# A forward long convolution as a software pipeline beside gate/up matmuls, with VectorE's operations held in program order

## The chip, the core and the metric

The kernel runs on one core of a Trainium2 chip. The metric is device time in microseconds for one execution. Five runs of the kernel before gave a median of 2061.96 us (2056.61 to 2076.34).

## What is computed

The reference computes a forward pass and the gradients of all its weights and of its input, for one sequence of S = 2048 positions and D = 1024 channels, in bfloat16. The forward pass, cut to what matters here:

```python
x  = A_q
xn = layernorm(x)                              # over the 1024 channels
k_shift = sum(k_pad[:, t:t + S, :] * shift_k[:, 3 - t] for t in range(4))
kv = k_shift * v
y  = irfft(rfft(kv) * rfft(ssm_k))[:S] + kv * ssm_D     # causal, per channel
s  = xn * y
g  = silu((xn @ w_gate) * (xn @ w_up) @ w_down)         # hidden width F = 3584
out = x + s * g
```

The long convolution is per channel and 2048 taps long. The backward pass (gradients for q, k, v, the two convolution kernels, D and the three weight matrices) takes the larger part of the time, and the change doesn't touch it.

## The kernel before, in words

The kernel works in stages on one core. Each stage has matrix work for TensorE that sets its pace, and a second stream of work, mostly for VectorE, that is fed in between its matmuls.

**The stage around the change** covers about the first 580 us. Its matrix work is the gate/up product: the 3584 hidden columns are cut into 14 weight slabs of 256 columns (for both matrices), each loaded by SP's queue into one of two buffers (`load_slab`, L488). `gu_unit` (L561) takes a slab and up to four blocks of 128 positions. For each block it runs eight matmuls of 512 columns into a PSUM tile (psg, two buffers; L569), and ScalarE copies the result into gut (L571). I call this a block below; the stage has 224 of them. At the end of the unit VectorE multiplies the two halves into hN (L575), GpSimd's queue stores hN to Hd (L576), and a deferred `turn` (L578) transposes it on TensorE (L583), copies it on ScalarE (L584), and stores it to HTd. `flush(5)` (L572) runs such deferred work five blocks later.

In the first 100 us slabs 0 and 1 are run on the rows as the layer norm delivers them, in chunks of 1, 1, 2, 4, 4 and 4 blocks of rows (L691, loop at L712). In this part the four rows of the shift kernel are also broadcast to all partitions (`bcast`, Wbc), and the cosine and sine tables of the transform are built (`build_tables`, L167).

**The convolution** is fed in from slab 2 on (`conv_forward`, L592). It works on eight slabs of 128 channels. For each pair of slabs, `shift` (L614) makes kv on VectorE in two halves: four products with Wbc, three additions, one product with v; the accumulator lies in U buffer 7. For each slab, `main` (L651) then runs:

- `h_rows` (L635): the convolution kernel's rows are transposed on TensorE and scaled on ScalarE to hx;
- `fwd4` (L226) on kv, then on hx: matmuls with the tables (psF, L221), a copy by ScalarE to SP (L236, two buffers), and then sums and differences on VectorE (first W from SP, then KX or HX from W);
- a store of KX to KFd and of HX to HFd, for the backward pass;
- `product` (L301): the complex product on VectorE, into KX;
- `inv_dft` (L335): sums on VectorE from KX back into HX.

`tail` (L668) ends a slab: inverse matmuls on HX (psY, `inv_rows`, L407, L415), a copy by ScalarE to yf (L673), and a store to YFd.

**What sets the order.** Each of these functions is a generator whose yields state how much VectorE work, in microseconds, was just issued. `make_pump` (L431) runs the generator until it has issued the wanted share of the total `F_TOTAL` (L689, 439.2 by its own sum); `tick` (L736) asks for one more 182.4th of it after each block. `staggered` (L450) mixes in the tail of the slab before, once 12 units of the present slab are out. This fixes the order in which the program is traced. A scheduler then orders each engine's instructions by when it expects them to be ready, so VectorE's order may differ from the traced one. `tc.issue_after(x)` is an order edge: what is traced in the block stands behind x on x's engine. All element-wise operations go through the helper `tt` (L198), so that VectorE's rows in the profile all show L199; they are told apart by their tiles.

## Time and profile before

| | before |
|---|---|
| median of five runs | 2061.96 us |
| the profiled execution | 2076.42 us |
| its span, first to last instruction | 2074.6 us |
| TensorE, mean granted clock | 0.979 |
| TensorE busy, 0 to 100 us | 81.5 us |
| TensorE busy, 100 to 582 us | 463.0 of 482 us |
| VectorE busy, 100 to 582 us | 411.4 of 482 us |
| ScalarE busy, 100 to 582 us | 251.3 of 482 us |

The profile is of one execution; the time beside the span in the table is that execution's own, and the 1.8 us between them lie outside the first and last instruction. PE is TensorE, DVE VectorE, ACT ScalarE, POOL GpSimd, SP the queue that issues most loads. In the rows, "out<-in" names the tiles, "xN" the number of instructions, and an arrow behind an idle time names what ended it. "Granted clock" is the share of TensorE's full clock that it was given.

### The profile page before, as it was taken

Reading aid. Unit: us, or ns where it says so; the run is one execution under the profiler, and the core shown is the slowest. Engines: PE = TensorE matmul, PEld = TensorE weight load, DVE = VectorE, ACT = ScalarE, POOL = GpSimd, SP = SyncE. Lnnn points to the kernel's source line nnn. Section 1 sums busy time; section 2 is a strip of 40 time slices with the busy share of each in tenths; the row PEclk is TensorE's granted clock in tenths of the full one; section 3 lists DMA queues with packets and bytes.
Section 4 is the critical chain, followed back from the end, with each engine's and each line's share of the span. In section 5 each row is a group of like instructions: output and inputs, shape, how many; then the busy total and the mean of one; then the engine's idle time right before and its main releaser. Section 6 shows DMA issues by size and latency. Waiting matters only on the chain.

```text
span 2074.6 us, 27733 instructions
## 1 busy us (share of the span) xinstructions
PE 1978.5 (95%) x11288; PEld 1057.3 (51%) x11288; DVE 1411.3 (68%) x1576; ACT 703.3 (34%) x962; POOL 304.5 (15%) x480
## 2 busy tenths in 40 slices
PE   6999999999999999999899899999999699999998
PEld 3455555545544446666555556654444344444443
DVE  6779898988836556887999889897473024434343
ACT  4655554546432233343222222334335001111112
POOL 3322222111112111000111221000000001010100
PEclk9999999999999999999999999999999899999999
DMA  9686656557699988665776676765999999393931
GB/s 297 213 270 220 215 206 219 186 187 248 228 293 291 290 290 255 200 218 198 265 249 202 222 244 218 238 231 164 173 224 177 186 206 224 100 194 98 209 96 56
DMA packets 422528, 440.74 MB, mean 212 GB/s; under 512 B 248960, under 2 KB 336824, under 8 KB 408576
## 3 DMA queue, kind: packets, MB, share of 16 engines
q1 hardware_dynamic: 331488, 203.72, 40.4%
q0 software_dynamic: 42112, 176.51, 25.5%
q10 hardware_dynamic: 48800, 58.73, 8.8%
q8 instruction: 88, 1.44, 0.3%
q14 instruction: 40, 0.33, 0.1%
HBM read 198.72 MB, written 189.83 MB: 187 GB/s over the span
## 4 chain that ended last, share of the span: by engine, by line
PE 39%; issue 30%; DVE 17%; DMA 6%; POOL 5%; ACT 2%; SPq 0%; POOLq 0%; ACTq 0%; DVEq 0%
PE psx L1224 16%; PE psb L1201 7%; PE psb L1100 6%; PE psg L569 5%; DVE W L199 5%; DVE m L199 3%; PE psb L1085 2%; DVE HX L199 2%; PE psF L221 1%; DVE A L199 1%; DVE U L199 1%; DMA B<-HFd 1%; DVE KX L199 1%; DVE B L199 1%; POOL out_dram L64 1%
## 5 line engine op out<-in xcount | busy, mean ns | idle before, releaser
L569 PE MATMUL psg<-wslab,U 128*128 128x512 bf16 x1792 | 419.1, 387 | 8.5 <-ACT U L542 5.0
L1100 PE MATMUL psb<-U,U 128*128 128x512 bf16 x1792 | 399.3, 383 | 13.4 <-DVE U L199 13.4
L1224 PE MATMUL psx<-U,dgut 128*128 128x512 bf16 x1536 | 339.3, 382 | 19.6 <-ACT wbs L1203 14.8
L1224 PEld LDWEIGHTS <-dgut 128*128 128x128 bf16 x1792 | 174.8, 98 | 233.3 <-issue 28.0
L1100 PEld LDWEIGHTS <-U 128*128 128x128 bf16 x1792 | 176.5, 99 | 224.0 <-issue 23.0
L569 PEld LDWEIGHTS <-U 128*128 128x128 bf16 x1792 | 175.8, 100 | 203.4 <-issue 18.3
L1085 PE MATMUL psb<-wdt,U 128*128 128x256 bf16 x1792 | 200.7, 273 | 1.1 <-ACT bm L979 1.1
L571 ACT CAST gut<-psg 128x512 bf16<-128x512 f32 x224 | 131.4, 587 | 206.5 <-PE psg L569 195.6
L1201 PE MATMUL psb<-U,U 128*128 128x512 bf16 x896 | 194.9, 379 | 6.0 <-ACT wbs L1203 4.4
L1085 PEld LDWEIGHTS <-U 128*128 128x128 bf16 x1792 | 176.0, 98 | 25.2 <-issue 1.4
L961 PE MATMUL psbm<-U,ht 128*128 128x512 bf16 x784 | 169.9, 379 | 0.0
L1105 ACT CAST wb<-psb 128x512 bf16<-128x512 f32 x112 | 66.4, 596 | 302.8 <-PE psb L1100 282.8
L199 DVE TENSOR_TENSOR W<-SP 128x1024 f32<-128x1024 f32 x96 | 113.0, 1220 | 69.4 <-ACT SP L236 37.8
L1201 PEld LDWEIGHTS <-U 128*128 128x128 bf16 x896 | 87.3, 98 | 111.1 <-issue 3.7
L199 DVE TENSOR_TENSOR dka<-dkh,Wbc 128x1024 bf16<-128x1024 bf16 x16 | 11.1, 692 | 193.0 <-DMA dkh<-DKSHd 193.0
L199 DVE TENSOR_TENSOR W<-W 128x1024 f32<-128x1024 f32 (+1 forms) x144 | 139.1, 984 | 2.8
L1247 ACT ACTIVATE dx_t<-dxn 128x1024 bf16<-128x1024 f32 (+1 forms) x17 | 17.1, 1007 | 348.8 <-DVE dxn L199 291.4
L199 DVE TENSOR_TENSOR m<-A,B 128x2048 bf16<-128x2048 bf16 (+1 forms) x48 | 73.2, 1575 | 84.1 <-issue 33.2
L961 PEld LDWEIGHTS <-ht 128*128 128x128 bf16 x784 | 76.6, 98 | 91.8
L1087 ACT CAST dht<-psb 128x512 bf16<-128x512 f32 x112 | 65.3, 586 | 130.3 <-PE psb L1085 110.1
L1203 ACT CAST wbs<-psb 128x512 bf16<-128x512 f32 x56 | 33.4, 622 | 146.6 <-PE psb L1201 80.8
L199 DVE TENSOR_TENSOR U<-U,dht 128x2048 bf16<-128x2048 bf16 x56 | 68.2, 1218 | 15.8 <-ACT dht L1087 15.8
(202 smaller groups left out, 2302.2 us busy)
## 6 DMA issues: line engine op xcount, KB each, us to landing
U<-GUd SPq DMA_DIRECT2D x28, 1024.0 KB, 7.3
DGd<-U SPq DMA_DIRECT2D x28, 1024.0 KB, 5.2
GUd<-gut ACTq DMA_DIRECT2D x54, 512.0 KB, 4.4
A<-DYFd POOLq DMA_DIRECT2D x16, 1024.0 KB, 6.6
out_dram<-wb ACTq DMA_DIRECT2D x112, 128.0 KB, 3.4
U<-Hd ACTq DMA_DIRECT2D x14, 1024.0 KB, 7.2
Hd<-hN POOLq DMA_DIRECT2D x54, 256.0 KB, 4.0
HTd<-hT POOLq DMA_DIRECT2D x54, 256.0 KB, 4.1
```

Of the source, the lines that this page charges most:

```text
L64: return nc.gpsimd.dma_start(out=out, in_=in_)
L199: V.tensor_tensor(o, a, b, op)
L569: gu_mm[0] = nc.tensor.matmul(ps[:], XNT[q][:, dc, qi * P:(qi + 1) * P], w[:, dc].rearrange("p a f -> p (a f)"), start=(dc == 0), stop=(dc ...
L571: nc.scalar.copy(out=gut[:, :, i], in_=ps[:].rearrange("p (a f) -> p a f", a=2))
L961: nc.tensor.matmul(ps[:, dh * 512:(dh + 1) * 512], ht(fc)[:, i * P:(i + 1) * P], WD[fc // 4][:, fc % 4, dh * 512:(dh + 1) * 512], start=(f ...
L1085: nc.tensor.matmul(ps[:, x * SLW:(x + 1) * SLW], DBMT[2 * hf + g][:, dc, (b % 4) * P:(b % 4 + 1) * P], wdt[:, dc, :], start=(dc == 0), sto ...
L1087: nc.scalar.copy(out=dht[:, 2 * e:2 * e + 2].rearrange("p b f -> p (b f)"), in_=ps[:])
L1100: nc.tensor.matmul(ps[:], XN[b // 4][:, b % 4, dc * P:(dc + 1) * P], dgus[b // 8][:, :, b % 8], start=(b == 0), stop=(b == NB - 1))
L1105: nc.scalar.copy(out=wb[:, dc % 2].rearrange("p a f -> p (a f)"), in_=ps[:])
L1201: nc.tensor.matmul(ps[:], h[:, b, f * P:(f + 1) * P], DBM[b // 4][:, b % 4, dh * 512:(dh + 1) * 512], start=(b == 0), stop=(b == NB - 1))
L1203: nc.scalar.copy(out=wbs[:, dh * 512:(dh + 1) * 512], in_=ps[:])
L1224: nc.tensor.matmul(ps[:, dh * 512:(dh + 1) * 512], t[n][:, f, i * P:(i + 1) * P], WGU[n][:, f, dh * 512:(dh + 1) * 512], start=(n == 0 and ...
```

## The change

1. VectorE is held in program order while the convolution runs: with `PIN[0]` set, every `tt` gets an order edge to the instruction traced before it on VectorE. It is set after the first shift product and cleared at the end of the stage.
2. `fwd4` is cut into `fwd4_half` (matmuls and ScalarE's copy of one half), `fwd4_sums` and `fwd4_outs` (VectorE). In the new loop the matmul halves are issued ahead: those of hx while VectorE works on kv's sums, those of the next slab's kv during the inverse sums (`ahead`).
3. The tail's four row pairs are issued one by one at fixed places in the next slab (`next(tl, None)`); the next slab's `h_rows` is issued before HX's last sums. `staggered` is no longer used here.
4. The shift product of the next pair stands between `product` and `inv_dft` of the odd slab, and the two halves of it use different accumulators (U 7 and U 6).
5. The first shift product (20 units) runs before slab 2; the rest is spread over the blocks. The statement of the work is new too (`F_TOTAL` 440.8).
6. hN is multiplied one block later, behind the copy of the next block, and its store and its turn are issued from there.
7. With the last two chunks of rows the order of the units is (4, slab 0), (5, slab 0), (4, slab 1), (5, slab 1) where it was (4, 0), (4, 1), (5, 0), (5, 1).

On SP's queue the order of one load changes: HT0[1][:, 0:8] from HTd now stands ahead of the pair of loads of slab 13. Behind the stage, all engines' orders stay as they were.

The core of the diff:

```diff
+    PIN = [False]
     def tt(o, a, b, op):
-        V.tensor_tensor(o, a, b, op)
+        ins = V.tensor_tensor(o, a, b, op)
+        if PIN[0]:
+            tc.keep_in_program_order(ins)
...
+    def fwd4_half(x, i, wp, psp, first=None):
+        SP = wp.tile([P, 2, 2, 512], F32, name="SP", bufs=2)
+        for par in range(2):
+            ps = psp.tile([P, 2, 2, 256], F32, name="psF")
+            cmm(ps[:, 0], T4[par], x, (i, i + 4), first if i == 0 else None)
+            cmm(ps[:, 1], T4[par], x, (i + 2, i + 6))
+            nc.scalar.copy(out=SP[:, :, par], in_=ps[:].rearrange("p s k x -> p s (k x)"))
+        return SP
+    def fwd4_sums(W, SP, i):
+        s, q = [SP[:, j].rearrange("p a (k x) -> p (a k) x", k=2) for j in range(2)]
+        tt(W[:, 0, i], s, q, ADD)
+        tt(W[:, 1, i], s, q, SUB)
...
             flush(5)
+            hn[0]()
+            hn[0] = nop
             tick()
         sta(GUd[sl, b0 // 8][:, :, b0 % 8:b0 % 8 + n], gut[:, :, 0:n])
-        tt(hN[:, 0:n], gut[:, 0, 0:n], gut[:, 1, 0:n], MUL)
-        st(Hd[sl][:, b0:b0 + n, :], hN[:, 0:n])
+        def multiply():
+            tt(hN[:, 0:n], gut[:, 0, 0:n], gut[:, 1, 0:n], MUL)
+            st(Hd[sl][:, b0:b0 + n, :], hN[:, 0:n])
+            defer(turn)
+        hn[0] = multiply
...
-                acc = U[7][:, 0:2048].rearrange("p (e r d) -> p e r d", e=2, r=8)
+                acc = U[7 - c][:, 0:2048].rearrange("p (e r d) -> p e r d", e=2, r=8)
...
+        yield from shift(0)
+        PIN[0] = True
+        yield 6.0
+        h_rows(0)
+        tl = iter(())
+        sp = [fwd4_half(kvs(0), i, cs, ps_cv) for i in range(2)]
         for ds in range(8):
-            yield from staggered(main(ds), tl, 12.0)
+            yield 0.5
+            W = fwd4_buf(cs)
+            fwd4_sums(W, sp[0], 0)
+            yield 2.4
+            fwd4_sums(W, sp[1], 1)
+            D0 = S_.pop(("D", ds))[:]
+            sph = [fwd4_half(S_["hx"], 0, cs, ps_cv, D0)]
+            yield 2.4
+            KX = cx.tile([P, 16, 256], BF16, name="KX")
+            fwd4_outs(KX, W, 0)
+            sph.append(fwd4_half(S_["hx"], 1, cs, ps_cv, D0))
+            yield 2.4
+            fwd4_outs(KX, W, 1)
+            st(KFd[ds], KX[:])
+            next(tl, None)
+            yield 2.4
+            W = fwd4_buf(cs)
+            for i in range(2):
+                fwd4_sums(W, sph[i], i)
+                next(tl, None)
+                yield 2.4
+            if ds < 7:
+                h_rows(ds + 1)
+            HX = cs.tile([P, 16, 256], BF16, name="HX", bufs=2)
+            for i in range(2):
+                fwd4_outs(HX, W, i)
+                next(tl, None)
+                yield 2.4
+            turned(HX, 1, 0, 1)
+            yield 1.3
+            st(HFd[ds], HX[:])
+            yield from product(KX, HX, KX, cs, False, 0)
+            if ds % 2 == 1 and ds < 7:
+                yield from shift(ds // 2 + 1)
+            sp = []
+            def ahead():
+                if ds < 7:
+                    sp.append(fwd4_half(kvs(ds + 1), len(sp), cs, ps_cv))
+            ahead()
+            yield from inv_dft(KX, HX, cs, ahead)
+            S_["G", ds] = HX
             tl = tail(ds)
...
-        for sl in range(2):
-            gu_unit(sl, b0, n, slabs[sl], nop)
-            if i in (3, 4):
+        for i_, sl in ([(i, 0), (i, 1)] if i < 4 else ([(4, 0)], [(5, 0), (4, 1), (5, 1)])[i - 4]):
+            gu_unit(sl, *xs[i_][0:2], slabs[sl], nop)
+            if i_ in (3, 4):
                 with tc.issue_after(gu_mm[0].ins):
-                    for j in ((3,), (2,), (1,), (0,))[2 * (i - 3) + sl]:
-                        bcast(j)
+                    bcast((3, 2, 1, 0)[2 * (i_ - 3) + sl])
...
     def tick():
         cnt[0] += 1
-        pump(cnt[0] / NT)
+        pump((20.0 + (F_TOTAL - 20.0) * cnt[0] / NT) / F_TOTAL)
+    pump(20.0 / F_TOTAL)
```

## The prediction

> **What bounds the kernel now.** I read the page first. TensorE is busy almost always, so time can only be won where it waits or runs at less than its full clock.

> ```profile
> PE 1978.5 (95%) x11288; PEld 1057.3 (51%) x11288; DVE 1411.3 (68%) x1576; ACT 703.3 (34%) x962; POOL 304.5 (15%) x480
> ```

> Nearly all the edits lie in the forward convolution, which shares 100 to 582 us with the gate/up matmuls (L569). So next: who TensorE waited for in that stretch.

> ```profile
> engine line waited for: us in total, times, longest us
> PE psY L415 <- DVE HX L199: 13.9, 5, 4.4
> PE psg L569 <- DMA wslab<-in_B_w_gate_dram: 3.0, 1, 3.0
> PE tr L583 <- ACT hT L584: 1.1, 1, 1.1
> PE tr L583 <- DVE hN L199: 0.8, 1, 0.8
> ```

> Two entries matter: the inverse transform's matmuls (psY) wait for VectorE's HX, and slab 2 of the weights once comes late. TensorE's timeline around one HX wait shows that the wait isn't all of it.

> ```profile
> 219.96 0.60 PE L415 MATMUL psY<-HX,TI 128*128 128x256 bf16 x4 [0.53 <-DVE HX L199]
> 220.39 2.97 PE L569 MATMUL psg<-wslab,U 128*128 128x512 bf16 x13
> 227.30 1.01 PE L415 MATMUL psY<-HX,TI 128*128 128x256 bf16 x4 [3.94 <-DVE HX L199]
> 230.67 1.91 PE L415 MATMUL psY<-HX,TI 128*128 128x256 bf16 x8
> 234.99 1.03 PE L415 MATMUL psY<-HX,TI 128*128 128x256 bf16 x8
> ```

> Eight of these matmuls take 1.91 us after the wait and 1.03 us a little later: half clock. The clock column (before "DMA share") of 7 us windows after the four long waits gives the price:

> ```profile
> 227.00:234.00 7.00, 6.70 (x35) 4.32 (x35) 6.86 (x7) 2.77 (x4) 2.78 (x5) 0.61 0.22 76
> 342.00:349.00 7.00, 6.15 (x24) 3.22 (x24) 6.84 (x6) 1.66 (x3) 0.09 (x1) 0.54 0.20 72
> 456.00:463.00 7.00, 7.00 (x31) 3.99 (x31) 0.21 (x1) 2.35 (x4) 0.00 (x0) 0.63 0.11 36
> 103.00:110.00 7.00, 6.79 (x31) 3.04 (x32) 2.62 (x3) 2.09 (x3) 2.36 (x4) 0.77 1.09 351
> ```

> 7 x (0.39 + 0.46 + 0.37 + 0.23) = 10.2 us. With the waits, 13.9 + 3.0, the two causes cost 27 us. That is nearly all that this change can win between 100 and 582 us; what lies behind 582 us keeps its order.

> **Durations.** I cost the change by start-to-start steps read from the timeline of before. TensorE: 0.216 us for 512 columns (32 of L569 last 7.07 us), 0.109 to 0.114 for 256, 0.056 for a transpose. VectorE: these rows (the last two figures ahead of "idle": busy us, mean ns).

> ```profile
> L199 DVE TENSOR_TENSOR W<-SP 128x1024 f32<-128x1024 f32 x64 | 75.1, 1219 | 37.9 <-ACT SP L236 37.8
> L199 DVE TENSOR_TENSOR HX<-W 128x1024 bf16<-128x1024 f32 x64 | 74.8, 1218 | 0.3
> L199 DVE TENSOR_TENSOR W<-KX 128x2048 f32<-128x2048 bf16 x16 | 36.6, 2287 | 0.3
> L199 DVE TENSOR_TENSOR U<-k,Wbc 128x2048 bf16<-128x2048 bf16 x24 | 29.3, 1220 | 6.2 <-DMA KSHd<-U 5.9
> ```

> Successive ones overlap by some 0.08 us (two HX<-W take 2.35 us), so a step is 1.14 us, 1.2 to 1.27 where the next needs it, 2.2 to 2.26 for the double ones, 0.60 for hN and turned.

> **Program order on VectorE, and the split of the forward transform.** No operation is added or removed, so each engine's work is unchanged. Two slabs of channels and one shift product take VectorE about 2 x 40.4 + 19.5 + 11.5 hN x 0.60 = 107 us. TensorE has 46 blocks of 8 x 0.216 = 79.5, psF and psY 192 x 0.11 = 21.5, and transposes and D rows 7.5 in the same span: 108.5 us. The engines are evenly matched; what decides is the order.

> The compiled order tells why before waits: psY of slabs 0 to 7 stands at blocks 65, 83, 110, 129, 156, 174, 202, 215, alternately 18 and 27 apart, while VectorE finishes HX every 57 us, since its scheduler spread the shift product over both slabs. From HX 0 to HX 1 VectorE needs 57 us, TensorE about 41. So I added each queue up in its order, with the steps above, stopping VectorE where hN or SP isn't there yet, and TensorE at HX. For before, HX leads psY by +10.5, -5.7, +8.7, -4.5, +8.3, -5.2, +9.9, -1.4 us. The trace waited 4.5 (0.53 + 3.94), 4.1, 4.4 and 0.8 us at the four negative ones and nowhere else. The sum is right in place and 0.4 to 1.2 us too pessimistic.

> For the changed order (psY at blocks 57, 84, 103, 131, 149, 177, 195, 213; the shift product now in one piece, so both engines have the long gap at the same place) the same sum gives +8.3, +7.7, +10.8, +8.6, +9.9, +9.4, +10.8, +1.5. Every HX wait goes: 13.9 us, and with it 7 x (0.39 + 0.46 + 0.37) = 8.5 us of clock.

> What is late next: the pipeline issues psF of the next slab's kv directly behind the shift product. On TensorE's order it comes 1.9, 2.2 and 1.9 us before VectorE has kv (slabs 2, 4, 6), and about 1.9 us at slab 0. Behind these psF matmuls in TensorE's queue stand gate/up blocks, so everything waits. Less the pessimism of 0.7 each: 4 x 1.3 = 5 us. The copy of hx's SP half waits until VectorE has read the kv half two before (two buffers); that comes out at 0.1 us three times, nothing.

> What no row shows is whether a wait of 1.3 us halves the clock. The nearest rows: waits of 0.8 to 1.1 us were followed by none, one of 2.96 us was (eight matmuls in 3.33 us where 1.89 is usual). [...] By the row the threshold is below 3 us, and each may cost up to 3.2 us more (the clock lost after an HX wait): 5 to 18 us. A gain is excluded, a wait can't speed anything. I take 7.5, near the short waits, with one of the four hit.

> **hN a block later, turn with it.** 54 multiplies, same work. They are traced behind the next block's copy, so VectorE's queue meets gut already copied; behind a waiting hN stand the convolution's sums, and in the sum above hN stops VectorE by at most 2.3 us. The transposes follow six blocks later (14 us); hN is at most 8 us late. The Hd and HTd stores move past KFd, HFd and YFd on GpSimd's queue. KFd and HFd must land (4.4 and 5.9 us) before VectorE overwrites KX and HX; the tightest, slab 2's HFd behind YFd and a turn, lands some 5 us before. Nothing, either way; if that cover is gone, VectorE stalls by the excess.

> **First shift product ahead of the pace; new pace.** 20 of 440.8 units run before slab 2, the rest at 2.31 instead of 2.41 per block. Its work hides beside the tables. Row 0 of the broadcast weights comes four blocks later, which is what makes the first kv late by 1.9 us (counted). The second accumulator (U 6) removes the KSHd wait of 5.9 us on VectorE, which was not on TensorE's path.

> **Slab 0 finished sooner.** Its last block moves from 28 to 24, so slab 2's load is issued 4 x 8 x 0.216 = 6.9 us sooner. It landed at 103.2 and was needed at 100.2; now about 96.3. Gone: 3.0 + 7 x 0.23 = 4.6 us. The fifth chunk of four rows is now needed at about 74.6 us, and its last transposed copy ended at 71.2, so it is there. If it weren't, each us would show.

> **HTd ahead of slab 13 on SP's queue.** That load now stands before slab 13's pair and waits for a turn at block 190; slab 13's buffer is free at 192 and it is needed at 200, 17 us later. It lands in 12 to 14. Covered by 3 to 5 us; without the cover, it is the excess plus the half clock, as at 103 us.

> **The sum.** 27.0 - 7.5 = 19.5. The profiled execution, 2076.4 us, would become 2056.9. The median of before is 14.5 us lower than that execution; I take the same difference off it: 2062.0 - 19.5 = 2042.5.

> **The rivals.**
> A, the forecast: 2036 to 2049, chance 0.57.
> B, no new wait: kv is in time, since the sum is pessimistic. Gain 27, 2035. For it: VectorE's waits for SP in before (37.8 us in all), which halves issued ahead can fill. Against it: four negative sums. 0.18.
> C, every kv wait halves the clock: 27 - 18 = 9, 2053; or the slab is all that is gained, 2057. For it: the 2.96 us row. 0.18.
> D, slower: VectorE, now strictly in order, becomes the bound. One operation that waits holds all behind it, and psF, hence the gate/up blocks, wait for kv at every second slab. It decides once VectorE's 107 us per two slabs grow by over 27 / 3.5 = 7.7 us (115 us); at 118 us it loses 10 us net, 2072. For it: 85% of VectorE is busy in the stage already (411 of 482 us). Against: no operation there showed more than 1.27 us. 0.07.

> Measurement tells about 0.5% from no change, 10 us: faster is below 2051.7. A and B lie there, with part of C: faster 0.80, same 0.14, slower 0.06. The range takes in B and most of C, with the spread of before's runs (2056.6 to 2076.3): 2030 to 2056.

> **What would show it.** Right: no psY wait for HX; the slab wait gone; psF waits for kv of 1 to 2 us at slabs 0, 2, 4 and 6; clock 0.99 or more between 100 and 582 us; stage shorter by about 20 us. Wrong: psF waits of 3 us or more with half clock behind them (C), VectorE busy without gaps over 95% (D), ScalarE's SP copies waiting for VectorE, or a wait for wslab near block 200.

## The result

The kernel after took 2061.14 us (median of 44 executions, 2039.46 to 2086.21) where the kernel before took 2069.62 (79 executions, 2049.04 to 2107.97) on the same chip. The ratio is 0.9955, 95% interval 0.9937 to 0.9974: 9 us gained, 5 to 13. The forecast was 2042.5 us and a gain of 19.5. The ratios leave out executions more than 1.5% above the fastest of their kernel; the means and standard deviations below are over all of them, and "either way" gives a 95% interval. The two means are 10.1 us apart, 4.5 either way.

The profiled execution of after took 2058.03 us, with a span of 2056.0. Its first row, which answers to the first line shown of before:

```profile
PE 1969.4 (96%) x11288; PEld 1053.4 (51%) x11288; DVE 1415.3 (69%) x1576; ACT 703.4 (34%) x962; POOL 305.0 (15%) x480
```

TensorE is busy 9 us less than in before (1978.5), with the same 11288 instructions. Eight psY matmuls of before took 1.91 us at half clock and 1.03 at full, so less busy time for the same work is clock won: the mean granted clock is 0.983 here, 0.979 in before. TensorE's waits in the forward stage, up to 582 us, as line, awaited operation, total, number of times, longest:

```profile
engine line waited for: us in total, times, longest us
...
PE psF L225 <- DVE kv L201: 6.4, 4, 2.2
...
PE tr L600 <- DVE hN L201: 1.3, 1, 1.3
PE tr L600 <- ACT hT L601: 1.1, 1, 1.1
PE psF L225 <- ACT SP L237: 0.5, 2, 0.3
```

No psY row waits for HX any more (13.9 us in before), and none waits for wslab (3.0). What is new is the first row, psF waiting for kv: 6.4 us in four waits, none over 2.2. The forecast had the place and the size (5 us, 1 to 2 each). TensorE's timeline at slab 2, then the stage and the 7 us after each long kv wait (TensorE's granted clock is the figure ahead of DMA share and GB/s):

```profile
209.83 2.42 PE L225 MATMUL psF<-kv,TF 128*128 128x256 bf16 x16 [1.97 <-DVE kv L201]
212.04 0.63 PE L580 MATMUL psg<-wslab,U 128*128 128x512 bf16 x1
212.46 2.90 PE L225 MATMUL psF<-kv,TF 128*128 128x256 bf16 x16
```

```profile
100.00:582.00 482.00, 472.28 (x2930) 265.08 (x2929) 416.51 (x366) 252.36 (x354) 106.59 (x163) 1.00 0.69 229
207.00:214.00 7.00, 5.03 (x29) 3.33 (x28) 6.90 (x7) 2.95 (x4) 4.64 (x7) 0.79 0.74 236
321.00:328.00 7.00, 4.82 (x38) 3.56 (x37) 6.90 (x6) 3.10 (x4) 3.54 (x6) 1.00 0.96 321
432.00:439.00 7.00, 5.03 (x39) 3.65 (x38) 6.90 (x7) 3.55 (x5) 2.00 (x3) 1.00 0.42 152
```

One of the three waits (207 us) is followed by half clock, two are not. Over 100 to 582 us the clock is 1.00 (0.98 in before) and TensorE is busy for 472.28 us (462.96 in before), so it does more of the work inside this window: the last gate/up matmul starts at 561.0 us, 578.1 in before. The stage gained 17.1 us in this pair of profiles. Nothing in the diff touches what comes behind, yet the measured gain of the kernel is 9. So two questions were open: how much the stage gains in an ordinary execution, and whether the rest takes some of it back.

### The profile page after: what moved, and what is told of

Read it like the earlier page. It is cut to its first block, busy times and chain, and to the rows that moved or that the text cites. A ratio compares the mean times of both kernels' runs of the same rounds, so it can differ in the third digit from the quotient of the medians.

```text
span 2056.0 us, 27710 instructions
## 1 busy us (share of the span) xinstructions
PE 1969.4 (96%) x11288; PEld 1053.4 (51%) x11288; DVE 1415.3 (69%) x1576; ACT 703.4 (34%) x962; POOL 305.0 (15%) x480
## 4 chain that ended last, share of the span: by engine, by line
PE 58%; DVE 18%; issue 11%; DMA 6%; SPq 3%; POOL 2%; ACT 2%; ACTq 0%; POOLq 0%; DVEq 0%
PE psx L1277 19%; PE psg L580 12%; PE psb L1153 8%; PE psb L1254 7%; DVE W L201 4%; DVE U L201 4%; DVE m L201 3%; PE psb L1138 3%; PE psF L225 3%; PE psbm L1014 2%; DVE A L201 2%; DMA out_dram<-wbs 2%; SPq L1220 1%; PE psY L423 1%; SPq L1213 1%
## 5 line engine op out<-in xcount | busy, mean ns | idle before, releaser
L580 PE MATMUL psg<-wslab,U 128*128 128x512 bf16 x1792 | 414.5, 383 | 4.8 <-ACT U L550 4.3
L1277 PE MATMUL psx<-U,dgut 128*128 128x512 bf16 x1536 | 340.3, 383 | 14.3 <-ACT wbs L1256 11.0
L1300 ACT ACTIVATE dx_t<-dxn 128x1024 bf16<-128x1024 f32 (+1 forms) x17 | 17.1, 1007 | 347.5 <-DVE dxn L201 293.2
L201 DVE TENSOR_TENSOR W<-SP 128x1024 f32<-128x1024 f32 x96 | 112.4, 1220 | 33.2 <-ACT SP L276 28.3
L201 DVE TENSOR_TENSOR U<-U,dht 128x2048 bf16<-128x2048 bf16 x56 | 68.2, 1218 | 15.1 <-ACT dht L1140 15.1
```

What stands on the lines that cost most here:

```text
L201: ins = V.tensor_tensor(o, a, b, op)
L580: gu_mm[0] = nc.tensor.matmul(ps[:], XNT[q][:, dc, qi * P:(qi + 1) * P], w[:, dc].rearrange("p a f -> p (a f)"), start=(dc == 0), stop=(dc ...
L1277: nc.tensor.matmul(ps[:, dh * 512:(dh + 1) * 512], t[n][:, f, i * P:(i + 1) * P], WGU[n][:, f, dh * 512:(dh + 1) * 512], start=(n == 0 and ...
```

## The experiments

Three theories stood at the start. **Theory 1**: the stage gains its 17 us in every execution, and the rest is spread of later stages. **Theory 2**: the profiled execution of before lost unusually much in this stage. **Theory 3**: the later stages give some 8 us back, because the change moves them against something. The runs fall into five groups, each on a chip of its own beside executions of before: both kernels again, slab 0's order and kv's psF later in the code; the forward stage and the eight buffers; plain loads and ScalarE's queue; the next three experiments; the last one. The mean of before was 2067.7, 2069.3, 2077.1, 2070.1 and 2064.2 us there.

**Both kernels again, unchanged.** No edit.

> The kernel before, unchanged, for a second profile. Theory 1 (the forward stage is 17 us shorter in every execution; the rest of the median's shortfall is spread of the later stages, which the change doesn't touch): the last gate/up matmul lies at 578 to 583 us again, with psY waits for HX of about 14 us in all, and the parts behind it differ from the first profile by up to 10 us either way. Theory 2 (the first profile showed an unusually bad forward stage): the last gate/up matmul lies at 573 us or sooner. Ratio 1.00.

Measured: 2072.86 us (12 executions, 2047.29 to 2095.45; ratio to the other executions of before 1.0021, 0.9978 to 1.0063). Last gate/up matmul at 579.5 us.

> The changed kernel, unchanged. Theory 1: the last gate/up matmul at 561 to 566 us again, psF waits for kv of 6 to 7 us, and later parts that differ from the first profile by up to 10 us either way; ratio anywhere from 0.988 to 0.999, about 17 us on the mean of many. Theory 2: the stage is at 563 us again but the kernel before comes closer to it. Theory 3 (the later stages lose what the forward stage won, because the change moves them against something): the parts behind the forward stage are longer by some 8 us than those of the kernel before in the same call.

Measured: 2051.3 us (12 executions, 2043.7 to 2083.14; ratio 0.9935, 0.9894 to 0.9975). Last gate/up matmul at 562.7 us. So the profiles repeat to 1.7 us in the forward stage, while whole executions of one kernel differ by up to 60 us. TensorE's waits behind 582 us show where, first in the first profile of after, then in its second:

```profile
PE psb L1254 <- ACT wbs L1256: 14.1, 1, 14.1
...
PE psx L1277 <- ACT wbs L1256: 11.0, 1, 11.0
```

```profile
PE psx L1277 <- ACT wbs L1256: 5.5, 1, 5.5
...
PE psb L1254 <- ACT wbs L1256: 2.3, 1, 2.3
```

These rows belong to the down-projection's weight gradient and the dx stage behind it: 25 us of waits in one execution, 8 in the other, of the same kernel (19 in the first profile of before). The change doesn't touch these stages.

**Slab 0's new order alone.** In before, only the loop over the last units is replaced:

```
-        for sl in range(2):
-            gu_unit(sl, b0, n, slabs[sl], nop)
+        for i_, sl in ([(i, 0), (i, 1)] if i < 4 else ([(4, 0)], [(5, 0), (4, 1), (5, 1)])[i - 4]):
+            gu_unit(sl, *xs[i_][0:2], slabs[sl], nop)
```

> The kernel before with nothing but the new order of the units of the last two chunks of rows (the last slab-0 unit ahead of a slab-1 unit). By the prediction: the wait for slab 2 is gone and with it 3.0 us and 1.6 us of clock, 4.6 us in all; the psY waits stay at about 14 us. Ratio 0.998. Rival: the later chunk of rows isn't ready or the broadcast row is late, and nothing is won.

Measured: 2069.5 us (ratio 0.9976, 0.993 to 1.0022). The wait for wslab is gone from its profile, the HX waits are all there (14.8 us). Its last gate/up matmul starts at 570.5 us, but a gain of a few us can't be told from the times in this spread.

**kv's psF later in the code.** In after, its two halves are called inside the inverse transform instead of ahead of it, and row 0 of the broadcast weights comes earlier:

```
-            ahead()
-            yield from inv_dft(KX, HX, cs, ahead)
+            yield from inv_dft(KX, HX, cs, ahead, ahead)
...
```

> The changed kernel with the next slab's kv matmuls issued two steps later (behind the first and the second half of the inverse sums) and the last broadcast row one unit sooner. By theory: the psF waits for kv (6.4 us in the profile of the changed kernel) go, with some 2 us of clock, and the forward stage ends at 554 to 558 us. Rival: VectorE then waits for SP at the head of the next slab by as much, HX comes later, and psY or psF waits come back: stage at 562 us or more.

Measured: 2052.3 us (ratio 0.9951, 0.9911 to 0.9991). The three long kv waits stayed at 6.1 us, and the stage ended at 559.8 us, not at 554 to 558. The compiled order tells why: psF of slab 2's kv stands behind block 78.9 in both kernels, since the scheduler places TensorE's instructions by its own estimate of when kv is ready. The edit moved lines of code and not the instruction, so it tells nothing about the three waits.

**The forward stage by itself.** Both kernels end behind the stage; the backward half is left out.

```
     for p_ in (ps_cv, ps_y, ps_tr, ps_gu, fg, fw):
         p_.release()
+    for p_ in (ua, tfp, tip):
+        p_.release()
+    return
```

> The kernel before, ended after the forward stage (its last gate/up block, transposes and stores); the backward half is left out, so that only outputs of the forward half are written. Two profiles of the whole kernel before have their last gate/up block at 578.1 and 579.6 us, so about 585 to 590 us here with the last turn and stores. This and the next run are a pair. Theory 1 (the forward stage gains the 17 us of the profiles in every execution, and the smaller gain of the whole kernel, 9.9 us between all 126 executions of before and all 56 of after, is the spread of the later stages): this is 16 to 18 us above its pair, and executions of it spread by few us. Theory 2 (the profiled executions of before lost unusually much in this stage): this is only 8 to 11 us above its pair. Theory 3 (the later stages give 7 to 8 us back): 16 to 18 us above its pair, as in theory 1; the other pair tells these two apart.

> The kernel after, ended at the same place, with the same part left out. Two profiles of the whole kernel after have the last gate/up block at 561.0 and 562.7 us. Theory 1 and theory 3: 16 to 18 us below its pair. Theory 2: 8 to 11 us below.

Measured: 586.73 us (5 executions, 580.57 to 588.28) and 572.19 us (4 executions, 570.58 to 573.61). The means are 13.0 us apart, 4.4 either way. Theory 2 has a part of the truth: the profiled pair of the whole kernels, with 17.1, was at the upper end. The waits of the forward-only profiles are those of the whole kernels (13.9 us for HX and 2.6 for wslab in one, 6.4 for kv in the other). What varies is the start: the 257th gate/up matmul comes at 98.2 us here, at 103.2 in the first profile of before.

**More buffers for the weight gradient's rows.** wbs is what TensorE waited for behind 582 us, so both kernels got eight buffers instead of four:

```
-    wo = pool("wo", 4, side="right")
+    wo = pool("wo", 8, side="right")
```

> The kernel before with 8 instead of 4 buffers for the rows of the down-projection's weight gradient on their way out (wbs), and no other edit; the order of every engine stays as it was. In six profiles the stage that fills them takes 207 to 236 us, and TensorE waits there for wbs for 0 to 24 us, since its stores stand behind transposing loads on SP's queue. If that is where executions differ, this kernel has its stage at 205 to 212 us, its median lies some 10 us below before's (about 2052 to 2060), and its executions spread less than before's (standard deviation about 12 us). If not, median and spread stay.

> The kernel after with the same 8 buffers. Theory 1 (the spread of the later stages hides the gain): with that spread cut, this is 16 to 18 us below its pair. Theory 2 (before's forward stage usually loses less than in its profiles) and theory 3 (the later stages give back 7 to 8 us): 8 to 11 us below its pair. Theory 3 has its loss in this stage, or where dx waits for it: then it is gone with the buffers, and the pair differs by 16 to 18 us only if both are measured at equal medians of the other stages.

Measured: 2056.77 us (10 executions, standard deviation 25; ratio to before 0.992, 0.9877 to 0.9963) and 2068.91 (12 executions, 13; ratio 0.9987, 0.9941 to 1.0032). The means are 3.3 us apart, 19 either way, and by the two ratios the order is even the reverse: the pair decides nothing, and the spread has not shrunk. The profile of the second shows that with more buffers TensorE waits for another late transfer, and still for wbs. First TensorE's timeline, then the load of the DMA queues from 1480 to 1530 us (queue, packets, MB, share of the 16 engines' time; then issues: transfer, KB, median us to landing):

```profile
1529.33 6.11 PE L1254 MATMUL psb<-U,U 128*128 128x512 bf16 x16 [15.68 <-DMA U<-Hd]
1545.64 4.85 PE L1254 MATMUL psb<-U,U 128*128 128x512 bf16 x11 [10.20 <-ACT wbs L1256]
```

```profile
q1 hardware_dynamic: 5104, 2.13, 72.7%
...
U<-Hd ACTq DMA_DIRECT2D x2, 1024.0 KB, 41.3
...
out_dram<-wbs SPq DMA_DIRECT2D x2, 256.0 KB, 42.0
```

Queue 1 carries what SP issues, the transposing loads of w_gate and w_up and the stores of wbs. It moves 2.13 MB in 50 us and takes 72.7% of the engines' time for it. Beside that, a load of 1 MB on ScalarE's queue (Hd) takes 41.3 us to land, and a store of wbs 42.0.

**The same loads made plain.** They bring the same bytes without transposing, so dx gets untransposed operands; the work and order of TensorE, VectorE, ScalarE and GpSimd are the same. In both kernels, and likewise for DGd:

```
-        nc.sync.dma_start_transpose(out=store, in_=(B_w_gate, B_w_up)[a][:, j * 512:(j + 1) * 512])
+        ld(store.rearrange("p a (h f) -> p (a h) f", f=512),
+           (B_w_gate, B_w_up)[a][:, j * 512:(j + 1) * 512].rearrange("(p x) f -> p x f", p=P))
```

> The kernel before with the transposing loads of w_gate, w_up and DGd for the last two stages made plain loads of the same bytes, so dx gets untransposed operands; order and work of TensorE, VectorE, ScalarE and GpSimd stay. In the profiles one such load holds SP's queue for 15 to 47 us while rows of a weight gradient and with them TensorE wait. If these loads are the source of the spread, the stage of the down-projection's weight gradient takes 200 to 206 us, executions differ by less than 5 us (standard deviation) and the median lies near 2030 to 2045. This and the next are a pair that compares the two kernels with little spread. Theory 1 (the gain of the forward stage reaches the end): 13 to 17 us above its pair. Theory 3 (later stages give some back whatever their spread): 8 to 10 us above. Theory 2, that the profiles of before are unusual, is weakened by the forward pair (13.1 us between the means, 11.8 to 16.7 between profiles).

> The kernel after with the same loads made plain. Theory 1: 13 to 17 us below its pair. Theory 3: 8 to 10 us below, and its dw, down-projection gradient or dx stage is longer than its pair's by the rest. Were it equal to its pair or slower, all theories would fall.

Measured: 2041.69 us (6 executions, standard deviation 4.7) and 2028.35 (6 executions, 2.8). The means are 12.8 us apart, 5.1 either way. Most of the spread is gone, and with it 29 us of the mean time of before (2069.8 over all its executions; 36, 8 either way, against those on this chip). The last gate/up matmuls of the two profiles are 12.3 us apart (574.5 and 562.2), the ends 13.1. Here are the last 603 us ahead of the final stores (us, busy time of PE and so on, with PE's clock third from the end), first of before's kernel, then of after's:

```profile
1427.00:1630.00 203.00, 202.99 (x1067) 96.97 (x1066) 107.54 (x106) 77.06 (x80) 8.22 (x14) 1.00 0.71 224
1630.00:2030.00 400.00, 399.62 (x2019) 184.17 (x2017) 155.31 (x207) 54.58 (x79) 38.54 (x61) 1.00 0.46 145
```

```profile
1414.00:1617.00 203.00, 202.99 (x1067) 96.94 (x1065) 107.44 (x106) 77.06 (x80) 8.22 (x14) 1.00 0.71 224
1617.00:2017.00 400.00, 399.49 (x2018) 184.04 (x2016) 155.83 (x207) 54.58 (x79) 38.53 (x61) 1.00 0.47 145
```

TensorE is busy for 202.99 of 203 us in both, at full clock. The same 13 us lie between the windows as lie between the kernels. So theory 3 falls where the transposing loads are taken out: nothing behind the stage gives anything back that shows. Theory 1 holds with 13 us in the place of 17.

**The stores of wbs on ScalarE's queue**, in both kernels, with the transposing loads as they were:

```
-            wst = ld(o_dwd[f0:f0 + P, :], wbs)
+            wst = sta(o_dwd[f0:f0 + P, :], wbs)
```

> The kernel before with the stores of wbs issued from ScalarE's queue instead of SP's, so that none stands behind a transposing load; nothing else edited (ScalarE's copies of yl move by a few places). If the spread of the later stages is this queueing, TensorE's waits for wbs (0 to 24 us) go, the median lies 8 to 15 us below before's, and the spread is cut. If the transposing loads slow all transfers, wbs or U<-Hd waits stay and so do median and spread.

> The kernel after with the same stores moved to ScalarE's queue. Theory 1: 13 to 17 us below its pair, at about 2040 if the queueing was the cause of the spread. Theory 3: 8 to 10 us below its pair. If all of this holds it is the fastest kernel so far.

Measured: 2082.22 us (ratio to before 1.0073, 1.0041 to 1.0105) and 2071.47 (ratio 1.0008, 0.9971 to 1.0046). The means are 13.0 us apart, 8.7 either way, as theory 1 had it. But the edit made nothing faster: the ratio of the first puts it 0.4 to 1.0% above before on the same chip (the means are 7.2 us apart, 8.9 either way), and TensorE waits 36 us for wbs in either. So a place in SP's queue is not all that the stores wait for. Around TensorE's longest wait for wbs in the first profile (17.3 us, to 1633.8), two loads of 352 KB on GpSimd's queue take 31 us beside transposing loads of DGd; over the whole profile their medians are 4.9 and 5.5. Whether the stores also stand behind the loads of Hd on ScalarE's queue was not tested.

With plain loads, single terms of the sum could be weighed, though against the plain pair on another chip: differences of 2 or 3 us decide little.

**Slab 0's order, plain loads** (the edit of the slab run above).

> The kernel before with plain loads (dx gets untransposed operands, as in the pair before) and the new order of slab 0's last units alone. If the slab's term was right (4.6 us), the median is about 2037 where the kernel before with plain loads had 2041.7; if only the late slab itself counts (waits of 2.6 to 3.3 us, mostly without half clock behind them), 2038.5 to 2039.5. The HX waits of 13.9 us stay, since nothing of the convolution is moved; psY's blocks stay at 65, 83, 110, 129.

Measured: 2038.84 us; the means are 2.2 us below the plain kernel before, 5.8 either way. The wait of 2.7 us for wslab is gone from the profile, and the last gate/up matmul starts 1.5 us sooner (573.0). The forecast's 4.6 is not excluded, half of it is nearer.

**After without VectorE's program order, plain loads.**

```
-        PIN[0] = True
+        PIN[0] = False
```

> The kernel after with plain loads, but VectorE's operations left to the scheduler (it mixes the last shift product's multiplies with the next channels' sums again; psY stays at blocks 57, 84, 103, 131, psF of kv moves from 79 to 77). If the program order is what removes the HX waits, they are back at every second slab, and the median is 2035 to 2042; if the pipelining and the shift product in one place do it, HX waits stay at zero, and the median is 2027 to 2031, or below 2027 if the order itself costs something.

Measured: 2030.56 us; the means are 2.3 us above the plain kernel after, 3.1 either way. TensorE's waits of the stage:

```profile
PE psF L225 <- ACT SP L237: 3.8, 1, 3.8
PE psF L225 <- DVE kv L201: 3.2, 1, 3.2
PE tr L600 <- DVE hN L201: 2.3, 1, 2.3
PE psY L423 <- DVE HX L201: 2.0, 1, 2.0
```

HX is late once (2.0 us), not 13.9 us in five waits. So most of the HX waits go with the rest of the change, whether or not the scheduler may shuffle VectorE. Nor is it the shift product in one piece: here VectorE spreads it over two slabs again, as in before (six of its products start between 165.0 and 233.8 us, in among the sums), and HX is in time everywhere else. What does differ from before in both kernels is how long VectorE waits for ScalarE's copies into SP, between 100 and 582 us: 37.8 us in before, and here in after and then without the order:

```profile
DVE W L201 <- ACT SP L237: 4.0, 1, 4.0
```

```profile
DVE W L201 <- ACT SP L237: 11.9, 7, 3.3
```

This points to the matmul halves issued ahead, but no run takes them out alone. Holding the order is worth some 2 us (the last gate/up matmul starts at 565.2 us without it, at 562.2 with it), and the interval reaches nought. Without it kv is late at slab 0 alone, so its three long waits come with the order.

**kv's psF really later.** In after, for slabs 2, 4 and 6, psF of kv comes behind the inverse transform, tied to VectorE's last operation there (`LAST[0]`, which `tt` keeps); it moves from block 78.9 to 81.0 at slab 2.

```
-            ahead()
-            yield from inv_dft(KX, HX, cs, ahead)
+            def late():
+                with tc.issue_after(LAST[0].ins):
+                    ahead()
+            if ds % 2 == 1 and ds < 7:
+                yield from inv_dft(KX, HX, cs)
+                late()
+                late()
+            else:
+                ahead()
+                yield from inv_dft(KX, HX, cs, ahead)
```

> The real kernel after with psF of the next slab's kv issued behind the inverse transform's last operation on VectorE at slabs 2, 4 and 6, so it stands 1.4 to 2.1 blocks (2.5 to 4 us) later in TensorE's order; VectorE's order is unchanged. The psF waits for kv (6.4 us in four) fall to under 1 us, and nothing takes their place, since VectorE needs the result some 4 blocks later. The forward stage ends at 552 to 556 us instead of 561 to 563. The whole kernel: 6 to 9 us below after, within a spread of 12 us; it is the candidate for the fastest.

> The same edit with plain loads. If the waits for kv cost what their time and the clock behind them add up to (6.4 plus 1.7 to 3.4 us), the median is 2019 to 2022, where the kernel after with plain loads had 2028.4. If VectorE is what paces the stage by then, so that a wait removed here comes back as a wait for HX, the median stays at 2026 to 2029.

Measured: the real kernel 2046.96 us (6 executions; ratio to before 0.9897, 0.9843 to 0.9951), with plain loads 2029.42. The plain means are 0.6 us above the plain kernel after, 4.2 either way. The gain expected of the real kernel's stage didn't come: it ends at 561.7 us (562.4 with plain loads), not at 552 to 556. As the other case had it, the wait came back, though at SP and not at HX. The waits of the plain profile, and the instructions around one:

```profile
PE psF L226 <- ACT SP L238: 7.3, 3, 2.6
...
PE psF L226 <- DVE kv L202: 0.3, 1, 0.3
```

```profile
219.34 4.62 DVE L202 TENSOR_TENSOR W<-SP 128x1024 f32<-128x1024 f32 x4
...
221.80 1.93 ACT L238 COPY SP<-psF 128x1024 f32<-128x1024 f32 x2 [4.18 <-DVE W L202]
222.87 3.26 PE L226 MATMUL psF<-hx,TF 128*128 128x256 bf16 x16 [2.34 <-ACT SP L238]
```

kv is late by 0.3 us in all, and psF of hx waits 7.3 us in three waits instead. ScalarE's copy into SP stands idle for 4.18 us until VectorE has read (W<-SP) the SP half two before. There are two SP buffers, and VectorE comes to that half only behind the shift product.

**The second half of hx later too.** On top of the last edit, for slabs 2, 4 and 6, this half moves from block 83 to 86:

```
-            sph.append(fwd4_half(S_["hx"], 1, cs, ps_cv, D0))
+            if ds not in (2, 4, 6):
+                sph.append(fwd4_half(S_["hx"], 1, cs, ps_cv, D0))
...
+            if ds in (2, 4, 6):
+                with tc.issue_after(LAST[0].ins):
+                    sph.append(fwd4_half(S_["hx"], 1, cs, ps_cv, D0))
```

> The kernel with psF of kv behind, and psF of the second half of hx 3 blocks later too (block 83 to 86 at slab 2, likewise at 4 and 6); VectorE's order is unchanged. If only the places were too early, the SP waits of 7.3 us go, no other comes (HX led psY by 8 to 11 us in the sum along the queues), and the forward stage ends at 553 to 556 us. If VectorE paces the stage, psY waits for HX instead and the stage still ends at 561 to 563. The whole kernel: in the first case 15 to 22 us below before, in the second as the kernel after.

> The same with plain loads. First case: median 2018 to 2022 (the kernel after with plain loads had 2028.4). Second case: 2026 to 2029.

Measured: the real kernel 2048.34 us (8 executions; ratio to before 0.9912, 0.9873 to 0.995), with plain loads 2023.53. The plain means are 3.0 us below the plain kernel after, 4.9 either way. The SP waits are gone, and a third wait has come (one of the four, of 0.2 us, lies in the first 100 us):

```profile
PE psg L581 <- ACT gut L583: 5.9, 4, 2.5
```

```profile
332.20 4.63 DVE L202 TENSOR_TENSOR W<-SP 128x1024 f32<-128x1024 f32 x4
...
334.65 1.93 ACT L238 COPY SP<-psF 128x1024 f32<-128x1024 f32 x2 [5.58 <-PE tr L601]
336.46 1.09 ACT L583 CAST gut<-psg 128x512 bf16<-128x512 f32 x2
...
337.12 0.59 PE L581 MATMUL psg<-wslab,U 128*128 128x512 bf16 x1 [2.50 <-ACT gut L583]
```

ScalarE's copy into SP still waits for VectorE. The profile names a transpose as its releaser, but it starts 2.45 us after W<-SP began, as in the profile above (2.46 us, 219.34 to 221.80), which is when two of the four W<-SP are done. The copy of the gate/up result (gut), which follows it on ScalarE, comes at 336.46, so the gate/up matmuls wait 2.50 us. Neither of the two cases was quite met: the stage ends at 558.5 and 560.5 us in the two profiles, not at 553 to 556 and not at 561 to 563. Of the 6.1 us of long kv waits, 5.6 are back.

In the real kernel the three later versions (2047, 2048 and 2052 us, 0.5 to 1% below before) can't be told from one another, nor from after.

## Why the forecast missed

Two steps failed: the median taken for before, from five executions, was some 7 us too low, and a third of the sum of 19.5 us was not there, since three small terms were mis-sized: the kv waits, slab 2's late load, and the stage's other small waits, which were put at nothing.

**Right: what bound the kernel, and what would be late next.** HX is no longer awaited, and psF waits for kv at slabs 2, 4 and 6 by 1.96 to 2.18 us in every profile of after (0.3 at slab 0). In the profile of after HX leads psY by 7.5, 8.6, 9.8, 8.6, 9.3, 9.3, 9.9 and 2.0 us, where the sum along the queues had 8.3, 7.7, 10.8, 8.6, 9.9, 9.4, 10.8 and 1.5. The load of slab 2 is never late. VectorE does not become the bound of rival D: nothing is slower. HTd on SP's queue and the stores cost nothing to be seen.

**Not shown: the reason for HX's lateness.** The forecast gave one, that the scheduler had spread the shift product over both slabs. Without the program order it is spread again, and HX waits 2.0 us instead of 13.9. The number came out; that cause does not suffice.

**The sum, term by term.** I summed, for every TensorE instruction, what its step to the next exceeded the median step of its kind by, in five whole traces of before's forward stage and five of after's:

- HX waits and the clock behind them: forecast 22.4 us, found 21.3 to 22.8. Right.
- kv waits and clock: forecast 7.5, found 8.1 to 9.7, mean 8.8. Short by 1.3. The sum along the queues gave 1.9, 2.2 and 1.9 us at slabs 2, 4 and 6, and 1.97, 2.17 and 1.96 came; the 0.7 taken off each for the sum's pessimism should have stayed on. The one at slab 0 was 0.3 instead of 1.9, so a wait too many made up for most of it: that the term came near is in part luck. Of the three, one or two were followed by half clock (one in the profile of after, two in the forward-only one).
- Slab 2: forecast 4.6, found 3.1 (3.7 of loss in before, 0.6 in after), because in three of the five profiles of before no half clock followed the late load, and it was not always as late. Short by 1.5.
- The rest of the stage, small waits as that for hN (1.0 in before, 1.5 in after): forecast nothing, found 1.1 of loss.

That makes 14 to 15. The last gate/up matmul starts 14.3 us earlier on average over these five pairs (17.1, 16.1, 14.3, 12.3, 11.8). The forward pair measured 13.0 and the plain pair 12.8. So the waits that go and come were the right ones, and of the 19.5 a third was not there: no term fell, but three small ones were mis-sized, all to the same side (3.9 us together; the rest of the way to 13 is within the intervals).

**Wrong: the step from the profile to the median.** "The median of before is 14.5 us lower than that execution; I take the same difference off it: 2062.0 - 19.5 = 2042.5." That median came from 5 executions. Over all 194 executions of before, these five among them, it is 2068.7, with a standard deviation of 13 us. So 7 us of the miss of 18.6 lie in the starting point. Another 6 lie in the sum (19.5 against 13). The rest, about 5, lies within the spread: over all of them, after (56 executions) has a mean 10.5 us below before, 3.7 either way, which 13 fits.

**Wrong: the range.** It took the spread from the same five executions (20 us wide), where 194 span 70. And I left the stages behind 582 us out, since their order is kept. Their order is, but not their duration: the down-projection's weight gradient takes 202 to 244 us in the profiles with transposing loads, and 202.3 in every one without (and in one of those with them).

**The rivals.** B (no new wait) is out: VectorE's waits for SP did shrink, from 37.8 to 4.0 us, but kv was late. C (every kv wait halves the clock) was the nearer one: 11 of 21 such waits did, each for 3.41 us, which costs 1.7 and not the 3.2 that C put on it. Its 2053 came out of a wrong starting point too. What none of them had is what the last runs showed: a wait that is taken away returns elsewhere, because with the shift product in one piece on VectorE, VectorE is 2 us behind TensorE at three places, and TensorE meets it at kv, at SP or at gut.

**Left open.** Whether the transposing loads cost the same on average beside either kernel was not settled, since the interval of the whole comparison (6.8 to 14.2 us) leaves room for a few us either way. Which part of the change brings HX in time was not taken apart. A third SP buffer, the direct way to give VectorE those 2 us, wasn't tried.

## What to carry to other kernels

Before forecasting a gain of 1%, find out how wide the executions spread and which stage makes the spread; one profile and five times do not show that. To measure a change of a few us, take the noisy stage away on both sides (end the kernel early, or make its transfers plain) rather than add executions: that cut the standard deviation from 13 to 5 us and less here. And where one engine runs level with another, a wait removed at one place is looked for at the next shared buffer.

## What was not expected of the hardware

**Lost clock came in steps, on a fixed grid.** In the 20 traces, 45 stretches of half clock (granted share 0.5) begin between 60 us and the end of the forward stage: 24 last 3.41 us, 21 last 6.83. At a share of 0.5 that costs 1.71 or 3.41 us at most, less what falls into the wait itself. None of 9 TensorE waits of 1.3 us was followed by one, 22 of 44 waits of 1.9 to 3.4 us were, and all 23 waits over 3.7 us. Here is the same wait of 2.17 us, in the kernel after and in its twin with plain loads:

```profile
324.03 1.91 PE L225 MATMUL psF<-kv,TF 128*128 128x256 bf16 x16 [2.17 <-DVE kv L201]
```

```profile
324.20 2.78 PE L225 MATMUL psF<-kv,TF 128*128 128x256 bf16 x16 [2.17 <-DVE kv L201]
```

**Transposing loads went with slow transfers on every queue.** They cost the kernel before 29 us or more and most of its spread (standard deviation 13 us, 4.7 with plain loads), though no engine computes less with plain ones. The same 50 us of the same stage as above, with plain loads:

```profile
q1 hardware_dynamic: 2677, 3.97, 21.6%
...
U<-Hd ACTq DMA_DIRECT2D x4, 1024.0 KB, 5.3
out_dram<-wbs SPq DMA_DIRECT2D x7, 256.0 KB, 5.4
```

Queue 1 moves 3.97 MB in 21.6% of the engines' time (2.13 MB in 72.7% with transposing), the 1 MB load of Hd lands in 5.3 us instead of 41.3, and the store of wbs in 5.4 instead of 42.0. On GpSimd's queue it is the same (KFd into B: 5.1 instead of 43.1). This is a bad stretch: in the first profile of before, in the same 50 us and with five such loads, Hd takes 9.0 us and wbs 6.5. A delay that varies like this fits the spread, and that neither more buffers nor another queue for the stores helped.
